# Loading q and k four units at a time, v's second slab by the batch, and identity made behind the first issues

## The chip, the cores and the metric

One core of a Trainium2 chip runs the whole program. The metric is the device time in microseconds of one execution; the median of three runs is compared. The profile is that of one execution, with its own time.

## The reference

Two stages, the output of the first being the input of the second. Batch 8, 8 heads, 576 positions, head size 64; chunks of 64 positions attend to themselves alone.

```python
scores = scale * np.matmul(q_c, k_c.transpose(0, 1, 2, 4, 3))   # per chunk: 64 x 64
scores = scores - np.max(scores, axis=-1, keepdims=True)
attn = np.exp(scores)
attn = attn / (np.sum(attn, axis=-1, keepdims=True) + 1e-09)
out = np.matmul(attn, v_c)                                      # per chunk: 64 x 64
...
x = out.transpose(0, 2, 1, 3).reshape(B, S, H * D)              # 8 x 576 x 512
wq = x @ w_q                                                    # 576 x 64
wk = x @ w_k
W_tok = scale * np.einsum('bsd,btd->bst', wq, wk)
mixed = np.einsum('bst,btd->bsd', W_tok, x)
return np.maximum(mixed, 0.0) @ w_out                           # 8 x 576 x 512
```

Inputs and output are float32 in HBM. The kernel works in float16 with float32 sums.

## The kernel before

**Units.** A batch has 8 heads of 9 chunks. The heads are taken in two slabs of four (slab 0: heads 0 to 3, slab 1: heads 4 to 7), so a batch has 36 chunk places, each with one chunk per slab. A unit is 8 places, that is 16 chunks; 36 units (`NU`) cover the 8 batches, and nine units cover a pair of batches. The fifth unit of the nine (`w == 4`) takes half of its places from each batch of the pair. v is cut otherwise: a batch has 18 slots of two places (`NS`), a unit uses four, and the two parts of a batch (`v_cuts`) hold slots 0 to 7 and 8 to 17.

**The loop.** Period `kk` of the main loop does, in the order in which the engines get it:

- `stage_b1(kk)`: TensorE computes the scores of unit kk (`sp`, L407), VectorE their row maximum (`mx`, L415). The pool of `sp` has one buffer.
- `stage_d1(kk-2)`: TensorE multiplies the transposed weights by v (`xp`, L452). v carries a column of ones, written by GpSimd's memset, so that the sum of the weights comes out as column 65.
- `fill(kk, 0, ...)`: steps of the second stage that a plan puts here.
- `stage_a1(kk+2)`: TensorE transposes q and then k of unit kk+2 (`tp`, L383, 16 instructions, eight for each). Then `loads(...)` gives GpSimd the loads that fall due.
- `stage_c(kk-1)`: TensorE transposes the exponentials (`ep`, L436); ScalarE copies them out (`et`).
- `stage_b2(kk)`: VectorE subtracts the maximum (`sh`, L421), ScalarE takes the exponential (`es`, L429).
- `stage_d2(kk-2)`: VectorE divides by the sum and writes `x_nat` (L464 to L467).
- `stage_a2(kk+2)`: VectorE copies the transposed q and k out of PSUM (`qkt`, L393).
- `fill(kk, 2, ...)`: steps of the second stage: transposes of `x_nat` (`tx`, L178), the products with w_q and w_k (L196), later the output product with w_out (`op`, L327), whose rows go out by SyncE.

A batch's second stage runs in the periods behind its attention. The first output product stands in period 13. Each engine works through its own instructions in program order and waits where an operand is not there.

**The loads.** All loads cast float32 to float16 and are issued by GpSimd, one queue, in program order. `load_qk(u)` loads unit u: one tile for q and one for k, each `[P, 2, R * D]`, one transfer of 128 KB each (256 rows of 512 bytes in float16); for the unit that straddles two batches, two transfers of 64 KB each. The tiles rotate over `AHEAD` = 8 buffers, so unit u waits until unit u-8 is transposed. `load_v(b, part)` loads a part of a batch's v: a memset of the ones, one transfer for slab 0 and two (the halves of the partitions swapped) for slab 1. Eight semaphores go round over GpSimd's transfers: a transfer is issued only when the eighth one before it has landed.

`wanted` holds all loads with the period at which each falls due; `loads(before)` issues those that are due before it. q and k of unit u are due at u-2, v's parts at two periods ahead of the unit that uses them first, w_q and w_k (`wqk16`) at 8, w_out (`wout16`) at 13; within a period v goes first, then q and k, then the weights:

```python
wanted = [(max(u - 2, 0), 1, load_qk, (u,)) for u in range(NU)]
...
wanted += [(8, 2, load_wqk, ()), (13, 2, load_wout, ())]
wanted.sort(key=lambda x: x[:2])
```

Identity (`ident`), which every transpose on TensorE reads, is made by two GpSimd instructions ahead of all loads.

Of the kernel before, what the change touches and what calls it, by code (L numbers as in the profile page):

```python
# [9 lines left out]
F16 = mybir.dt.float16  # L10
# [7 lines left out]
def kernel(  # L18
# [16 lines left out]
    nc = tc.nc  # L35
    B, H, S, D = q.shape
    DM = moe_w_out.shape[0]
    DH = moe_w_q.shape[1]
    CH = 64
    P = 128  # L40
    HQ = H // 2
    NC_ = S // CH
    NI = HQ * NC_
    NS = NI // 2
    NU = B * NI // 8
    W0 = 5 * CH
    R, G = 4, 16
    AHEAD = 8
# [2 lines left out]
    ds = bass.ds  # L51

    const = ctx.enter_context(tc.tile_pool(name="const", bufs=1))
    qn_pool = ctx.enter_context(tc.tile_pool(name="qn", bufs=AHEAD))
    v_pool = ctx.enter_context(tc.tile_pool(name="vpool", bufs=3))
    qkt_pool = ctx.enter_context(tc.tile_pool(name="qkt", bufs=3))
    sm_pool = ctx.enter_context(tc.tile_pool(name="smp", bufs=3))
# [12 lines left out]
    ctx.enter_context(tc.manual_schedule())  # L70

    ident = const.tile([P, P], F16, name="ident")
    make_identity(nc, ident[:])

    x_nat = const.tile([P, B * NS, 2, D], F16, name="x_nat")
    x_bat = x_nat[:].rearrange("p (b w s) l d -> p b w s l d", b=B, w=2)
# [1 line left out]
    wqk16 = const.tile([P, HQ, 2 * DH], F16, name="wqk16")  # L78
    wout16 = const.tile([P, HQ, DM], F16, name="wout16")

    v_cuts = ((0, 8), (8, NS))
    data = {}

    def load_qk(u):
        pair, w = divmod(u, 9)

        if w == 4:
            pieces = ((2 * pair, 32, 0, CH), (2 * pair + 1, 0, CH, CH))
        else:
            odd = int(w > 4)  # L90
            pieces = ((2 * pair + odd, 8 * w - NI * odd, 0, P),)
        for ti, x in enumerate((q, k)):
            tl = qn_pool.tile([P, 2, R * D], F16, name=f"qn{ti}", tag=f"qn{ti}")
            for b, i0, p0, pn in pieces:
                of = x[b].rearrange("h s d -> (h s) d").rearrange("(l p r) d -> p l (r d)", l=2, r=R)
                at = i0 * G
                nc.gpsimd.dma_start(tl[p0 : p0 + pn], of[at : at + pn])  # L97
            data[u, ti] = tl

    def load_v(b, part):  # L100
        n0, n1 = v_cuts[part]
        vt = v_pool.tile([P, 2, n1 - n0, D + 2], F16, name=f"vt{part}", tag=f"vt{part}")
        of = v[b].rearrange("h s d -> (h s) d").rearrange("(l n p) d -> l p n d", l=2, p=P)
        nc.gpsimd.memset(vt[:, :, :, D : D + 1], 1.0)

        for sl, to, at, rows in ((0, 0, 0, P), (1, 0, CH, CH), (1, CH, 0, CH)):
            nc.gpsimd.dma_start(vt[to : to + rows, sl, :, 0:D], of[sl, at : at + rows, n0:n1, :])  # L107
        data[b, part, 2] = vt

    def w_rows(w):  # L110
        return w.rearrange("(l i d) j -> l d i j", l=2, i=HQ)
# [10 lines left out]

    wanted = [(max(u - 2, 0), 1, load_qk, (u,)) for u in range(NU)]
    for b in range(B):
        for part in range(2):
            first = (NS * b + v_cuts[part][0]) // 4
            wanted.append((first + 2, 0, load_v, (b, part)))
    wanted += [(8, 2, load_wqk, ()), (13, 2, load_wout, ())]  # L130
    wanted.sort(key=lambda x: x[:2])

    def loads(before):
        while wanted and wanted[0][0] < before:
            _, _, load, args = wanted.pop(0)
            load(*args)

    loads(AHEAD - 2)

    drain = [False]  # L140
# [300 lines left out]
    def stage_d1(u):  # L441
        et = state[u]["et"]
        xp = x_psum.tile([P, 2, 512], F32, name="xp", tag="xp")
        xv = xp[:, :, 0 : 4 * 65].rearrange("p l (m e) -> p l m e", e=65)
        for m in range(4):
            b, s = divmod(4 * u + m, NS)
            part = s >= v_cuts[1][0]
            vt = data[b, part, 2][:, :, s - v_cuts[part][0]]
            for sl in range(2):
                for par in range(2):  # L450
                    at = CH * (par ^ sl)
                    nc.tensor.matmul(  # L452
                        xv[CH * par : CH * par + CH, sl, m, :],
                        lhsT=et[at : at + CH, m, CH * sl : CH * sl + CH],
                        rhs=vt[at : at + CH, sl, 0 : D + 1],
                        start=True,
                        stop=True,
                    )
        state[u]["xv"] = xv
# [21 lines left out]
    for b in range(B):  # L481
        period = lambda slots: -(-slots // 4) + 1
# [32 lines left out]
    for kk in range(NU - 1):  # L515
        stage_b1(kk)
        if kk >= 2:
            stage_d1(kk - 2)
        fill(kk, 0, 0.0)
        if 2 <= kk < NU - 2:  # L520
            stage_a1(kk + 2)
            loads(kk + 1 + AHEAD)
        if kk >= 1:
            stage_c(kk - 1)
        stage_b2(kk)
        if kk >= 2:
            stage_d2(kk - 2)
        if 2 <= kk < NU - 2:
            stage_a2(kk + 2)
        for u in ((1,), (2, 3))[kk] if kk < 2 else ():  # L530
            stage_a(u)
        fill(kk, 2, 1.4 if len(outs) < 4 else 1.9)
# [17 lines left out]
    u = NU - 1  # L550
    stage_b1(u)
    stage_d1(u - 2)
    stage_c(u - 1)
    stage_b2(u)
# [5 lines left out]
    chain(B - 2, 2)  # L560
    stage_c(u)
    stage_d1(u - 1)
    stage_d2(u - 1)
    put()
# [47 lines left out]
```

## Time and profile before

| | |
|---|---|
| runs | 150.97, 152.11, 152.70 us; median 152.11 |
| the profiled execution | 151.31 us, its span 149.5 us |
| TensorE's granted clock, mean | 0.957 |
| busy: TensorE (matmul) | 125.4 us, 84% of the span |
| busy: VectorE | 113.6 us, 76% |
| busy: ScalarE | 101.0 us, 68% |
| busy: GpSimd (POOL) | 98.0 us, 66% |
| GpSimd's loads of v (L107) | 48 transfers, 828 ns each |
| GpSimd's loads of q and of k (L97) | 40 and 40 transfers, 744 and 741 ns each |
| packets of GpSimd's queue | 58,976; 14.82 MB |

The span is the time from the first to the last instruction; the rest of an execution's time lies around it. GpSimd's busy time is that of issuing a transfer; the transfer lands some microseconds later. The page cuts the span into 40 slices of 3.74 us and gives each engine's busy share in tenths, so a 9 means 90% or more; the DMA row is the mean share of the 16 transfer engines. A timeline line gives start, duration, engine, line, operation, tiles written and read, and in brackets the idle time of the engine just before and what ended it.

### The profile page before, as it was taken

How to read it: one execution, taken by the hardware profiler on the slowest of the kernel's cores; microseconds unless marked ns; L12 is line 12 of the kernel's file. 1: busy time of each engine (PE TensorE's matmuls, PEld its weight loads, DVE VectorE, ACT ScalarE, POOL GpSimd, SP SyncE). 2: the span in 40 equal slices, each digit the busy share in tenths (PEclk: the TensorE clock that was granted, in tenths of full speed). 3: DMA queues.
4: the chain of work that ended last, by engine and by line, in shares of the span. 5: the costliest groups of instructions: out<-in, count | busy, mean ns of one | idle time of the engine just before them, and what ended most of it. 6: DMA issues, size and time to landing. Idle time of an engine off the chain costs nothing.

```text
span 149.5 us, 5958 instructions
## 1 busy us (share of the span) xinstructions
PE 125.4 (84%) x2516; PEld 84.5 (57%) x2516; DVE 113.6 (76%) x235; ACT 101.0 (68%) x199; POOL 98.0 (66%) x156
## 2 busy tenths in 40 slices
PE   0477898678789499999999999999899988999970
PEld 0256667556656265676756656765667554544430
DVE  0169998999999448998999899979989897354520
ACT  3013347368589529997898898879979996677130
POOL 7999999989999589879966997599650000000000
PEclk9999757999999869999999999999999999999996
DMA  2999999999999999999999999999999433234484
GB/s 19 140 149 158 140 158 154 162 90 139 164 136 141 170 181 199 224 215 201 219 172 226 188 199 246 221 163 227 208 215 138 129 147 148 76 140 119 167 269 153
DMA packets 64875, 25.09 MB, mean 168 GB/s; under 512 B 40784, under 2 KB 60368, under 8 KB 64848
## 3 DMA queue, kind: packets, MB, share of 16 engines
q0 software_dynamic: 58976, 14.82, 104.7%
q1 hardware_dynamic: 5728, 9.75, 19.3%
q8 instruction: 20, 0.33, 0.9%
q10 hardware_dynamic: 144, 0.13, 0.3%
q14 instruction: 7, 0.06, 0.1%
HBM read 29.62 MB, written 9.44 MB: 261 GB/s over the span
## 4 chain that ended last, share of the span: by engine, by line
PE 40%; POOL 17%; DVE 14%; ACT 13%; DMA 7%; issue 6%; DVEq 0%; ACTq 0%; POOLq 0%
PE op L327 13%; POOL qn L97 11%; PE tp L383 5%; DMA wout<-in_moe_w_out_dram 5%; POOL vt L107 4%; DVE sh L421 4%; PE ep L436 3%; DVE x_nat L467 3%; DVE mx L415 3%; PE sp L407 3%; ACT osb L154 3%; PE gp L250 3%; DMA qn<-in_k_dram 3%; ACT es L429 3%; PE tx L178 3%
## 5 line engine op out<-in xcount | busy, mean ns | idle before, releaser
L107 POOL DMA_DIRECT2D vt<-in_v_dram x48 | 38.1, 828 | 2.8 <-issue 1.8
L438 ACT COPY et<-ep 128x512 f16<-128x512 f16 x36 | 21.6, 600 | 19.2 <-PE ep L436 17.9
L383 PE MATMUL tp<-ident,qn 128*64 128x128 f16 x576 | 26.7, 239 | 7.7 <-DMA qn<-in_q_dram 4.8
L327 PE MATMUL op<-wout,rmx 128*128 128x512 f16 x124 | 31.4, 387 | 2.1 <-DMA wout<-in_moe_w_out_dram 1.9
L97 POOL DMA_DIRECT2D qn<-in_k_dram x40 | 29.4, 741 | 5.2 <-PE wpb L196 1.0
L97 POOL DMA_DIRECT2D qn<-in_q_dram x40 | 29.5, 744 | 3.0 <-DMA qn<-in_q_dram 0.9
L415 DVE TENSOR_REDUCE mx<-sp 128x8 f32<-128x512 f32 x36 | 24.7, 685 | 8.2 <-PE sp L407 8.2
L393 DVE COPY qkt<-tp 128x1024 f16<-128x1024 f16 x36 | 24.5, 682 | 6.7 <-PE tp L383 6.6
L429 ACT ACTIVATE es<-sh 128x512 f16<-128x512 f32 x36 | 23.4, 651 | 7.6 <-DVE sh L421 7.6
L421 DVE TENSOR_TENSOR sh<-sp,mx 128x512 f32<-128x512 f32 x36 | 24.9, 692 | 3.5
L383 PEld LDWEIGHTS <-qn 128*64 128x64 f16 x576 | 20.5, 120 | 12.3 <-DMA qn<-in_q_dram 4.8
L467 DVE TENSOR_TENSOR x_nat<-xp,rec 128x512 f16<-128x512 f32 x36 | 24.9, 692 | 1.2
L154 ACT COPY osb<-op 128x512 f32<-128x512 f32 (+1 forms) x29 | 17.1, 598 | 9.5 <-PE op L327 8.0
L407 PEld LDWEIGHTS <-qkt 64*64 64x64 f16 x576 | 12.8, 115 | 13.9 <-issue 4.9
L407 PE MATMUL sp<-qkt 64*64 64x64 f16 x576 | 17.0, 203 | 2.8 <-DVE qkt L393 1.9
L154 ACT COPY xt<-tx 128x768 f16<-128x768 f16 (+1 forms) x23 | 18.2, 790 | 0.9 <-PE tx L178 0.9
L327 PEld LDWEIGHTS <-rmx 128*128 128x128 f16 x124 | 11.2, 99 | 12.5 <-issue 3.2
L452 PE MATMUL xp<-vt,et 64*64 64x65 f16 x576 | 12.8, 201 | 5.5 <-DVE x_nat L467 2.6
L160 ACT ACTIVATE rmx<-ma 128x512 f16<-128x512 f32 x28 | 15.6, 622 | 0.1
L436 PE MATMUL ep<-ident,es 128*128 128x128 f16 x144 | 14.9, 229 | 0.0
L452 PEld LDWEIGHTS <-et 64*64 64x64 f16 x576 | 9.3, 110 | 7.3 <-ACT es L429 2.9
L178 PE MATMUL tx<-ident,x_nat 128*128 128x128 f16 x144 | 12.3, 223 | 0.0
(47 smaller groups left out, 141.4 us busy)
## 6 DMA issues: line engine op xcount, KB each, us to landing
out_dram<-osb SPq DMA_DIRECT2D x31, 256.0 KB, 3.5
qn<-in_q_dram POOLq DMA_DIRECT2D x32, 128.0 KB, 5.1
qn<-in_k_dram POOLq DMA_DIRECT2D x32, 128.0 KB, 5.4
vt<-in_v_dram POOLq DMA_DIRECT2D x8, 160.0 KB, 5.7
vt<-in_v_dram POOLq DMA_DIRECT2D x16, 80.0 KB, 5.4
out_dram<-osb SPq DMA_DIRECT2D x9, 128.0 KB, 2.4
vt<-in_v_dram POOLq DMA_DIRECT2D x8, 128.0 KB, 6.6
vt<-in_v_dram POOLq DMA_DIRECT2D x16, 64.0 KB, 5.9
```

The lines of the kernel that those rows point to most:

```text
L97: nc.gpsimd.dma_start(tl[p0 : p0 + pn], of[at : at + pn])
L107: nc.gpsimd.dma_start(vt[to : to + rows, sl, :, 0:D], of[sl, at : at + rows, n0:n1, :])
L154: (nc.vector.tensor_copy if on_vector else nc.scalar.copy)(to, of)
L327: nc.tensor.matmul(op[:], lhsT=rmx[:, i, ds(t * P, P)], rhs=wout16[:, i, :], start=(i == 0), stop=(i == HQ - 1),)
L383: nc.tensor.transpose(tp[CH * sl : CH * sl + CH, ti, :, r, :], src[:, sl, r * D : r * D + D], ident[:],)
L393: nc.vector.tensor_copy(qkt[:].rearrange("p t c k -> p (t c k)"), tp[:].rearrange("p t c r g -> p (t c r g)"),)
L407: nc.tensor.matmul(sp[rows, i ^ sl, :], lhsT=qkt[rows, 0, i, :], rhs=qkt[rows, 1, i, :], start=True, stop=True,)
L415: nc.vector.tensor_reduce(mx[:], sp[:], axis=AX.X, op=ALU.max)
L421: nc.vector.tensor_tensor(out=sh[:].rearrange("p i (g r) -> p i g r", g=G, r=R), in0=sp[:].rearrange("p i (r g) -> p i g r", g=G, r=R), in ...
L429: nc.scalar.activation(es[:], sh[:], AF.Exp, scale=scale_attn)
L452: nc.tensor.matmul(xv[CH * par : CH * par + CH, sl, m, :], lhsT=et[at : at + CH, m, CH * sl : CH * sl + CH], rhs=vt[at : at + CH, sl, 0 : ...
L467: nc.vector.tensor_tensor(out=x_nat[:, 4 * u : 4 * u + 4, :, :].rearrange("p m l d -> p l m d"), in0=xv[:, :, :, 0:D], in1=rec[:, :, :, No ...
```

## The change

- From unit 9 on (the third batch), q and k are loaded by fours: units 9 to 12, then 13 alone, 14 to 17, then 18 to 21, 22, 23 to 26, and so on. A group's tile is `[P, 2, 4, R * D]`, and one transfer brings one slab of four units of q or of k: 256 KB, 512 rows of 512 bytes. A group of four units is four transfers (q slab 0, q slab 1, k slab 0, k slab 1) in place of eight, and falls due when its first unit did before. Units 0 to 8 are still loaded one by one, into tiles of the same shape. The tiles of four rotate over three buffers; those of the straddling units have their own.
- v has one tile per batch. From the third batch on slab 1 is loaded whole, in two transfers (the two halves of the partitions, 18 slots each), with the first part of slab 0. The second part of slab 0 falls due where it did. There is one memset per batch.
- Unit 0's two transfers are issued ahead of identity's two instructions; the other loads follow behind these.

With that the issue order behind unit 8 becomes: units 9 to 12; v of batch 1, second part; w_q and w_k; v of batch 2, first part of slab 0 and slab 1 whole; unit 13; units 14 to 17; v of batch 2, second part of slab 0; w_out; v of batch 3 likewise; units 18 to 21; and so on. Before it was: unit 9; v of batch 1, second part; unit 10; w_q and w_k; units 11 and 12; v of batch 2, first part; units 13 and 14; v of batch 2, second part; unit 15; w_out; unit 16; and so on.

```diff
-    qn_pool = ctx.enter_context(tc.tile_pool(name="qn", bufs=AHEAD))
+    qn_pool = ctx.enter_context(tc.tile_pool(name="qn", bufs=3))
...
     ident = const.tile([P, P], F16, name="ident")
-    make_identity(nc, ident[:])
...
-    def load_qk(u):
+    def load_qk(u, n):
         pair, w = divmod(u, 9)
-        if w == 4:
-            pieces = ((2 * pair, 32, 0, CH), (2 * pair + 1, 0, CH, CH))
-        else:
-            odd = int(w > 4)
-            pieces = ((2 * pair + odd, 8 * w - NI * odd, 0, P),)
         for ti, x in enumerate((q, k)):
-            tl = qn_pool.tile([P, 2, R * D], F16, name=f"qn{ti}", tag=f"qn{ti}")
+            if w == 4:
+                tl = qn_pool.tile([P, 2, 1, R * D], F16, name=f"qm{ti}", tag=f"qm{ti}")
+                pieces = ((2 * pair, 32, 0, CH), (2 * pair + 1, 0, CH, CH))
+            else:
+                odd = int(w > 4)
+                if w in (0, 5):
+                    tiles[ti] = qn_pool.tile([P, 2, 4, R * D], F16, name=f"qn{ti}", tag=f"qn{ti}")
+                at = w - 5 * odd
+                tl = tiles[ti][:, :, at : at + n]
+                pieces = ((2 * pair + odd, 8 * w - NI * odd, 0, P),)
             for b, i0, p0, pn in pieces:
                 of = x[b].rearrange("h s d -> (h s) d").rearrange("(l p r) d -> p l (r d)", l=2, r=R)
-                at = i0 * G
-                nc.gpsimd.dma_start(tl[p0 : p0 + pn], of[at : at + pn])
-            data[u, ti] = tl
+                g0 = i0 * G
+                if n == 1:
+                    nc.gpsimd.dma_start(tl[p0 : p0 + pn, :, 0], of[g0 : g0 + pn])
+                    continue
+                for sl in range(2):
+                    nc.gpsimd.dma_start(
+                        tl[:, sl], of[g0 : g0 + n * P, sl].rearrange("(t p) x -> p t x", p=P)
+                    )
+            for j in range(n):
+                data[u + j, ti] = tl[:, :, j]
-    def load_v(b, part):
-        n0, n1 = v_cuts[part]
-        vt = v_pool.tile([P, 2, n1 - n0, D + 2], F16, name=f"vt{part}", tag=f"vt{part}")
+    def load_v(b, sl, n0, n1):
+        if not (sl or n0):
+            data[b] = v_pool.tile([P, 2, NS, D + 2], F16, name="vt", tag="vt")
+            nc.gpsimd.memset(data[b][:, :, :, D : D + 1], 1.0)
...
-    wanted = [(max(u - 2, 0), 1, load_qk, (u,)) for u in range(NU)]
+    wanted = [(max(u - 2, 0), 1, load_qk, (u, 1)) for u in range(9)]
+    for u in range(9, NU, 9):
+        wanted += [(u + w - 2, 1, load_qk, (u + w, n)) for w, n in ((0, 4), (4, 1), (5, 4))]
     for b in range(B):
-        for part in range(2):
-            first = (NS * b + v_cuts[part][0]) // 4
-            wanted.append((first + 2, 0, load_v, (b, part)))
+        for part, (n0, n1) in enumerate(v_cuts):
+            period = (NS * b + n0) // 4 + 2
+            wanted.append((period, 0, load_v, (b, 0, n0, n1)))
+            if b < 2:
+                wanted.append((period, 0, load_v, (b, 1, n0, n1)))
+            elif part == 0:
+                wanted.append((period, 0, load_v, (b, 1, 0, NS)))
...
+    load_qk(*wanted.pop(0)[3])
+    make_identity(nc, ident[:])
     loads(AHEAD - 2)
```

More of the change, by code (lines that the diff above doesn't have):

```diff
@@ L81 @@
     v_cuts = ((0, 8), (8, NS))
-    data = {}
-    def load_qk(u):
+    data, tiles = {}, {}
+    def load_qk(u, n):
         pair, w = divmod(u, 9)
-        if w == 4:
-            pieces = ((2 * pair, 32, 0, CH), (2 * pair + 1, 0, CH, CH))
-        else:
-            odd = int(w > 4)
-            pieces = ((2 * pair + odd, 8 * w - NI * odd, 0, P),)
-        for ti, x in enumerate((q, k)):
-            tl = qn_pool.tile([P, 2, R * D], F16, name=f"qn{ti}", tag=f"qn{ti}")
+        for ti, x in enumerate((q, k)):
+            if w == 4:
[8 more added lines that the diff above has]
+                pieces = ((2 * pair + odd, 8 * w - NI * odd, 0, P),)
@@ L103, in load_v @@
+                for sl in range(2):
[8 more added lines that the diff above has]
+            nc.gpsimd.memset(data[b][:, :, :, D : D + 1], 1.0)
         of = v[b].rearrange("h s d -> (h s) d").rearrange("(l n p) d -> l p n d", l=2, p=P)
-        nc.gpsimd.memset(vt[:, :, :, D : D + 1], 1.0)
@@ L106, in load_v @@
-        for sl, to, at, rows in ((0, 0, 0, P), (1, 0, CH, CH), (1, CH, 0, CH)):
-            nc.gpsimd.dma_start(vt[to : to + rows, sl, :, 0:D], of[sl, at : at + rows, n0:n1, :])
-        data[b, part, 2] = vt
+        for to, at, rows in ((0, CH, CH), (CH, 0, CH)) if sl else ((0, 0, P),):
+            nc.gpsimd.dma_start(
+                data[b][to : to + rows, sl, n0:n1, 0:D], of[sl, at : at + rows, n0:n1, :]
+            )
     def w_rows(w):
@@ L446, in stage_d1 @@
             b, s = divmod(4 * u + m, NS)
-            part = s >= v_cuts[1][0]
-            vt = data[b, part, 2][:, :, s - v_cuts[part][0]]
+            vt = data[b][:, :, s]
             for sl in range(2):
```

## The prediction

> **What bounds the kernel now.** I read the slices first, then VectorE's timeline, then the chain of waits at the gaps, then the issue and transfer rows of the loads.
>
> ```profile
> DVE  0169998999999448998999899979989897354520
> POOL 7999999989999589879966997599650000000000
> DMA  2999999999999999999999999999999433234484
> ```
>
> The DMA engines are busy from the first microseconds to about 115 us; GpSimd (POOL), which issues every load, is full until 45 us. VectorE is at 9 or more in most slices, with a hole at slices 13 and 14. Its timeline there (start, duration, line, count, idle before):
>
> ```profile
> 47.18 0.68 DVE L415 TENSOR_REDUCE mx<-sp 128x8 f32<-128x512 f32 x1
> 47.97 0.69 DVE L421 TENSOR_TENSOR sh<-sp,mx 128x512 f32<-128x512 f32 x1
> ...
> 49.61 0.68 DVE L393 COPY qkt<-tp 128x1024 f16<-128x1024 f16 x1
> 54.10 0.69 DVE L415 TENSOR_REDUCE mx<-sp 128x8 f32<-128x512 f32 x1 [3.80 <-PE sp L407]
> ```
>
> One L415 runs per unit, so I call its start for unit u mx(u). mx(12) is at 44.16, mx(13) at 47.18, a pitch of 3.03 us in which VectorE never rests: that is the loop's bound. mx(14) comes 3.80 us late. The chain of waits says why:
>
> ```profile
> 44.62 6.87 DMA wout<-in_moe_w_out_dram
> 51.49 0.14 issue
> 51.62 1.86 PE op L327 x4
> 53.49 0.46 PE sp L407 x6
> ```
>
> TensorE works in program order. It had finished everything ahead of L327 at 49.73, waited 1.89 us for the output weights, which land at 51.49, and only then reached unit 14's scores. With the weights there, L327 takes 0.86 us (its row at 56.28), so mx(14) would have come at about 51.05: the late weights cost 3.0 us. After that mx(17) is at 63.62 and no later group of rows waits for a load. The 30 us behind the loop are not touched.
>
> The margin of the loads is small everywhere:
>
> ```profile
> 28.90 0.64 PE L383 MATMUL tp<-ident,qn 128*64 128x128 f16 x16
> 29.47 0.40 PE L436 MATMUL ep<-ident,es 128*128 128x128 f16 x4
> 29.70 0.50 PE L178 MATMUL tx<-ident,x_nat 128*128 128x128 f16 x6
> 30.55 0.44 PE L407 MATMUL sp<-qkt 64*64 64x64 f16 x16 [0.35 <-DVE sh L421]
> ```
>
> Unit 9 is transposed (L383) at 28.90, its k half at 29.2. Its k was issued at 23.02 and, by the 4.7 us that loads take there, is in SBUF at 27.6. Three rows price the transfer engines (window, us; busy us and counts by engine; clock; DMA share; GB/s):
>
> ```profile
> 24.90:26.50 1.60, 1.10 (x46) 0.81 (x42) 1.60 (x3) 1.44 (x3) 1.60 (x4) 1.00 1.24 154
> 45.60:51.50 5.90, 3.80 (x83) 2.62 (x81) 4.45 (x11) 4.65 (x11) 4.88 (x8) 0.98 1.14 147
> 54.00:56.00 2.00, 2.00 (x50) 1.65 (x43) 1.73 (x5) 0.48 (x2) 1.27 (x3) 0.82 1.48 191
> ```
>
> 154 GB/s where q and k alone move behind a short queue, 191 behind a full one, 147 around the output weights.
>
> **Identity.** Its two GpSimd instructions take 0.74 to 1.44 and now stand behind unit 0's two issues. Unit 0's q goes out 0.70 us sooner; TensorE's first transpose, at 4.59 before, starts at 3.9, and identity is ready at 0.74 + 2 x 0.71 + 0.70 = 2.9. If that cover of 1.0 us were gone, the first transpose would slip by what is missing. Every later issue keeps its time. The gain ends at unit 6, still issued at 16.48:
>
> ```profile
> 16.48 4.00 DMA qn<-in_k_dram
> 20.48 0.04 issue
> 20.52 0.64 PE tp L383 x8
> ...
> 22.95 0.70 DVE mx L415
> ```
>
> mx(5) hangs on that landing, and its time does not change. Bounds 0 and -0.7; I take 0.
>
> **GpSimd's issues.** Twenty-four units lose 8 transfers per four (0.71 us apart) and get 4 of 512 rows each. No row shows a 512-row q or k transfer. Bounds: 0.71 (a 256-row transfer) and 1.42 (twice that); v's 640-row transfers take 0.72 and its 1280-row one 0.98, so 0.77. Six batches lose four v half transfers (2 x 0.69, 2 x 0.72) and get two of about 0.84. Together 24 x 1.42 - 24 x 0.77 + 6 x 1.14 = 22 us less on GpSimd, and eight memsets of 0.24 fewer. On the path that is worth nothing by itself: after unit 8 the transfer engines set the pace, at either bound of the price. The tile waits do not bind either: units 18 to 21 reuse the tile of 5 to 8, transposed long before.
>
> **The move.** Up to unit 8 both orders are the same; its k is issued at 21.60 and lands 4.7 us later, at 26.3. Behind it now come units 9 to 12 as four transfers, 1.05 MB, and unit 9's k half waits for the last one, three units' bytes more than before. At 172 GB/s, halfway between 154 and 191 (the queue is now deeper than in the first row), that is 6.1 us: landing 32.4, against a need at 29.2. TensorE stops in front of L383 for 3.2 us; queued behind it are L436, L178 and unit 8's L407. From the landing these need 0.3 + 0.4 + 0.5 + 0.44 us; at unit 6 the same steps took 2.47, so I take 2.0: mx(8) at 34.4, not 32.04, a loss of 2.4. The slab-0 rest of v of batch 1, then wqk, land behind the group, at about 34.3 and 35.1, where TensorE now needs them at 34.1 and 35.2: no second wait beyond a few tenths.
>
> Next is wout. Ahead of it: v of batch 1 (0.33 MB), wqk (0.13), v of batch 2 without the end of slab 0 (0.43), unit 13 (0.26), units 14 to 17 (1.05), the end of slab 0 (0.16): 2.36 MB, 13.7 us; wout itself 0.52 MB at 147 GB/s, 3.6 us. It lands at 49.7; TensorE wants it at 49.73 + 2.4 = 52.1. So the wait of 1.89 goes, and mx(14) = 47.18 + 2.4 + 3.03 + 0.85 = 53.5, against 54.10: 0.6 us gained. Units 14 to 17 land at about 45.1, needed at 44.6 + 2.4.
>
> Next is the group 18 to 21. Behind wout come 0.43 MB of v and 1.05 MB: 0.7 MB until 53.9, when stores begin, and then 0.75 MB with two stores of 0.26 at about 205 GB/s (between 192 and 209, what 51.5 to 61.5 and 61.5 to 95.1 moved): 6.2 us, landing 60.1. Unit 18's k is needed 2.35 us ahead of mx(17), at 60.6. At 165 GB/s in place of 172 the same steps give 61.2 to 62.5 (two or three stores) and mx(17) between 63.6 and 64.9. The later groups have margins of 1 to 3 us on the same count.
>
> Sum at mx(17): between -0.65 and +1.2 us, middle +0.3. Profiled execution: 151.31 us (span 149.5, 1.8 around it), so 151.6; the median of the runs, 152.11, is 0.8 above it: **152.4 us**, no change within 1%, which is about what a measurement of this kernel can tell.
>
> **Rivals.** *The groups land late (slower).* Place: TensorE in front of L383 of units 9 and 18. Price: at 150 GB/s units 9 to 12 land at 33.3 (mx(8) +3.3), wout at 52.7, just in time, units 18 to 21 at about 64, and mx(17) = 66.3, +2.7; 0.1 to 0.3 more at a later group. It decides below about 160 GB/s. For it: 154 and 147 above, and the waits of TensorE for q and k that are there already. Against: those rows had short queues, or the output weights in them. Time 155.1.
>
> *The queue runs full (faster).* At 191 GB/s units 9 to 12 land at 31.8 (mx(8) +1.8), wout at 47.8, units 18 to 21 before they are needed: mx(14) is 1.25 early and stays so. With 0.5 us less chain behind the landing (1.5 by the sum of its rows) it is 1.75. For it: the row of 191, and that GpSimd no longer starves the queue between 26 and 45 us. Against: that rate held for 2 us. Time 150.5.
> [...]
>
> *The change does not do what it says:* a 512-row issue costs 1.42 or more. Then the fourth transfer is issued at 22.3 + 3 x 1.42 = 26.6 and lands, at 4.7 + 0.7 us, at 32.0, inside the forecast; it is part of it.
>
> **Chances.** Forecast 0.39, slower rival 0.37 (154 to 156), faster rival 0.24 (149.8 to 150.6). The forecast's own range is 151.0 to 153.6. Taking in both rivals' prices and the runs' spread (150.97 to 152.7): 149.9 to 156.0. So faster by over 1%: 0.24, within 1%: 0.39, slower by over 1%: 0.37.
>
> **What would show it.** Right: TensorE waits about 3 us for qn near 29 to 32 us and mx(8) is at 34 to 35; no wait for wout; mx(14) at 53 to 54; GpSimd busy about 76 us. The first transpose at 3.9 with mx(5) still near 22.9. Wrong: units 9 to 12 land before 30 (no wait), or a wait of over 2 us before unit 18, or L327 waiting for wout again.

## The result, and the profile after

The changed kernel takes 159.94 us (median of 4 runs, 159.11 to 160.69) against 152.19 us (4 runs, 150.97 to 152.70) on the same chip: ratio 1.053, 95% interval 1.045 to 1.060. It is slower by 5%, outside the range of the prediction. The profiled execution took 159.11 us, its span is 157.3 us, 7.8 more than before. Here and below, ratios are of the undisturbed runs on both sides, so they can differ a little from the ratio of the medians.

The slices of the page of after:

```profile
DVE  0378889927799788978793799988998997535630
POOL 7999999669973783677663469100000000000000
PEclk9999999965999999999996999999999999999997
DMA  3999999999999999999999999997121333243574
```

GpSimd has the room that was forecast (74.7 us busy instead of 98.0), and the transfer engines are as full as before, but for less long: the last load lands at 108.6 us, 115.3 before. VectorE, which set the pace, now has deep holes at slices 8 and 21 and shallow ones at 9, 10, 13, 17 and 19 (the first slice is slice 0). The clock falls at slices 8, 9 and 21. The starts of L437 (the old L415, `mx`) on VectorE's timeline show where the holes come from; the columns are start, duration, what it is, and in brackets the idle time before it:

```profile
35.58 0.69 DVE L437 TENSOR_REDUCE mx<-sp 128x8 f32<-128x512 f32 x1 [1.06 <-PE sp L429]
...
40.11 0.69 DVE L437 TENSOR_REDUCE mx<-sp 128x8 f32<-128x512 f32 x1 [1.41 <-PE sp L429]
...
53.33 0.69 DVE L437 TENSOR_REDUCE mx<-sp 128x8 f32<-128x512 f32 x1 [0.99 <-PE sp L429]
...
56.89 0.69 DVE L437 TENSOR_REDUCE mx<-sp 128x8 f32<-128x512 f32 x1 [0.44 <-PE sp L429]
...
80.74 0.68 DVE L437 TENSOR_REDUCE mx<-sp 128x8 f32<-128x512 f32 x1
...
87.09 0.69 DVE L437 TENSOR_REDUCE mx<-sp 128x8 f32<-128x512 f32 x1 [2.34 <-PE sp L429]
```

These are units 8, 9, 13, 14, 21 and 22. Before, they were at 32.04, 35.07, 47.18, 54.10, 76.38 and 79.41. So 3.5 us are lost at unit 8, 1.5 more at unit 9, some is won back at 14, and 3.3 are lost at 22. Each time TensorE is what VectorE waits for. TensorE's timeline at the first loss:

```profile
29.25 0.24 PE L405 MATMUL tp<-ident,qn 128*64 128x128 f16 x1
30.10 0.41 PE L405 MATMUL tp<-ident,qn 128*64 128x128 f16 x7 [0.60 <-DMA qn<-in_q_dram]
31.43 0.24 PE L405 MATMUL tp<-ident,qn 128*64 128x128 f16 x1 [0.92 <-DMA qn<-in_k_dram]
33.16 0.63 PE L405 MATMUL tp<-ident,qn 128*64 128x128 f16 x7 [1.49 <-DMA qn<-in_k_dram]
...
35.69 1.07 PE L405 MATMUL tp<-ident,qn 128*64 128x128 f16 x16
```

Unit 9 waits three times (for q's second slab and for each slab of k) for the four transfers of units 9 to 12, until 33.16. Then the same row of 16 transposes takes 1.07 us where it took 0.64: the granted clock is 0.50 from 33.5 to 36 us and 0.57 on average from there to 40 us, and for this while TensorE, not VectorE, sets the pace. The output weights, late before, are waited for no more. What comes after that has no load in its brackets:

```profile
49.30 0.25 PE L405 MATMUL tp<-ident,qn 128*64 128x128 f16 x2
51.03 0.58 PE L405 MATMUL tp<-ident,qn 128*64 128x128 f16 x14 [1.48 <-issue]
...
57.25 0.28 PE L473 MATMUL xp<-vt,et 64*64 64x65 f16 x11 [0.34 <-issue]
...
64.46 0.32 PE L473 MATMUL xp<-vt,et 64*64 64x65 f16 x16 [1.36 <-DVE mx L437]
...
80.88 0.58 PE L405 MATMUL tp<-ident,qn 128*64 128x128 f16 x14
83.72 0.30 PE L405 MATMUL tp<-ident,qn 128*64 128x128 f16 x2 [2.26 <-issue]
...
84.35 0.47 PE L218 MATMUL wpa<-xt,wqk 128*128 128x320 f16 x1
```

At 83.72 TensorE stops in the middle of a row of transposes of data that had been there for long (14 of its 16 were done), and "issue" says that no semaphore released it. At 51.03 it stops so too, ahead of transposes of unit 14's q, which had landed at 46.06; but of this unit's k the second slab lands only at 50.66, so a wait of about 1 us for k would have stood there without the stop. The stop at 64.46 bears the name of VectorE's `mx`, but L473 does not read `mx`; it is of the same kind (below). Behind the longest one the clock is halved again (L218 takes 0.47 us, 0.30 before). The same place before:

```profile
76.52 0.64 PE L383 MATMUL tp<-ident,qn 128*64 128x128 f16 x16
77.09 0.40 PE L436 MATMUL ep<-ident,es 128*128 128x128 f16 x4
77.33 0.30 PE L196 MATMUL wpa<-xt,wqk 128*128 128x320 f16 x1
```

Counted over all of TensorE's instructions in the trace (weight loads, matmuls and the few of its sequencer), these four stops and one of 0.36 us at 75.92 have 1473, 1729, 1985, 2753 and 2497 instructions before them: exactly 256 apart, or a multiple of it. (The pairs 747, 876, 1005 and 1391 of an expectation below are the matmuls and the sequencer's instructions counted together, to within one; the matmuls alone are 726, 853, 980 and 1362.) The page's queues have a row that fits:

```profile
q8 instruction: 20, 0.33, 0.8%
...
qn<-in_k_dram POOLq DMA_DIRECT2D x12, 256.0 KB, 8.4
vt<-in_v_dram POOLq DMA_DIRECT2D x12, 144.0 KB, 10.1
```

The row of q8 is twenty packets of 16,384 bytes (0.33 MB) of instructions, 64 bytes for each of 256; the page counts them with the loads, as a share of the same 16 transfer engines. TensorE has 5077 instructions in this trace, 19.8 times 256. The packets that start at 48.32, 54.72, 61.70 and 81.42 end 1.3 to 1.6 us before the four stops do. The last two of these rows are the median time from issue to landing: k's groups and v's take 8 to 10 us, where single units took 5.4 before and v's parts 5.4 to 6.6. The queue of loads beside an instruction packet is deeper than it was: by the issues and landings in the trace, up to 1.1 MB of loads (1 MB is 1024 KB here) were on their way before, and up to 1.6 or 1.7 MB in the 8 us ahead of each of these four packets.

### The profile page after: what moved, and what is told of

It is laid out like the page before. It is cut to its first block, busy times and chain, and to the rows that moved or that the text cites. A ratio compares the mean times of both kernels' runs of the same rounds, so it can differ in the third digit from the quotient of the medians.

```text
span 157.3 us, 5872 instructions
## 1 busy us (share of the span) xinstructions
PE 129.1 (82%) x2516; PEld 87.9 (56%) x2516; DVE 114.4 (73%) x235; ACT 101.6 (65%) x199; POOL 74.7 (47%) x112
## 4 chain that ended last, share of the span: by engine, by line
PE 45%; POOL 15%; DVE 14%; DMA 9%; ACT 8%; issue 6%; DVEq 0%; ACTq 0%; POOLq 0%
PE op L349 13%; POOL qn L103 7%; PE tp L405 6%; DMA qn<-in_k_dram 5%; POOL vt L119 4%; PE ep L458 4%; DVE x_nat L488 4%; DVE sh L443 4%; DMA wqd<-wqkT 3%; DVE mx L437 3%; PE tx L200 3%; PE wpa L218 3%; PE sp L429 3%; PE xp L473 2%; PE wknp L253 2%
## 5 line engine op out<-in xcount | busy, mean ns | idle before, releaser
L405 PE MATMUL tp<-ident,qn 128*64 128x128 f16 x512 | 25.2, 246 | 11.9 <-DMA qn<-in_q_dram 5.4
L437 DVE TENSOR_REDUCE mx<-sp 128x8 f32<-128x512 f32 x36 | 24.7, 687 | 12.6 <-PE sp L429 12.5
L119 POOL DMA_DIRECT2D vt<-in_v_dram x36 | 31.1, 905 | 5.0 <-DMA vt<-in_v_dram 2.0
L415 DVE COPY qkt<-tp 128x1024 f16<-128x1024 f16 x36 | 24.6, 683 | 9.1 <-PE tp L405 9.0
L349 PE MATMUL op<-wout,rmx 128*128 128x512 f16 x124 | 30.5, 379 | 0.2 <-ACT rmx L182 0.2
L405 PEld LDWEIGHTS <-qn 128*64 128x64 f16 x512 | 19.3, 124 | 15.9 <-DMA qn<-in_q_dram 5.9
L473 PE MATMUL xp<-vt,et 64*64 64x65 f16 x576 | 13.8, 204 | 6.5 <-DVE x_nat L488 2.8
L458 PE MATMUL ep<-ident,es 128*128 128x128 f16 x144 | 16.0, 241 | 0.0
L473 PEld LDWEIGHTS <-et 64*64 64x64 f16 x576 | 10.0, 112 | 8.2 <-ACT es L451 2.9
L200 PE MATMUL tx<-ident,x_nat 128*128 128x128 f16 x144 | 13.2, 233 | 0.4 <-issue 0.4
L106 POOL DMA_DIRECT2D qn<-in_q_dram x12 | 9.4, 813 | 4.4 <-DMA qn<-in_k_dram 1.9
L106 POOL DMA_DIRECT2D qn<-in_k_dram x12 | 9.1, 777 | 4.8 <-PE gp L272 1.0
```

The costliest lines, as they stand in the source:

```text
L119: nc.gpsimd.dma_start(data[b][to : to + rows, sl, n0:n1, 0:D], of[sl, at : at + rows, n0:n1, :])
L349: nc.tensor.matmul(op[:], lhsT=rmx[:, i, ds(t * P, P)], rhs=wout16[:, i, :], start=(i == 0), stop=(i == HQ - 1),)
L405: nc.tensor.transpose(tp[CH * sl : CH * sl + CH, ti, :, r, :], src[:, sl, r * D : r * D + D], ident[:],)
L415: nc.vector.tensor_copy(qkt[:].rearrange("p t c k -> p (t c k)"), tp[:].rearrange("p t c r g -> p (t c r g)"),)
L437: nc.vector.tensor_reduce(mx[:], sp[:], axis=AX.X, op=ALU.max)
L458: nc.tensor.transpose(ep[:, m, :], es[:, 2 * m : 2 * m + 2, :], ident[:])
```

## Experiments

The account up to the end of the loop, from the starts of `mx` in each profiled execution (us; the last column is the difference of the two before it):

| kernel | unit 9 | unit 14 | unit 17 | unit 35 | 17 to 35 |
|---|---|---|---|---|---|
| before | 35.07 | 54.10 | 63.62 | 120.72 | 57.10 |
| after | 40.11 | 56.89 | 67.51 | 128.37 | 60.86 |
| before, with q and k by fours alone | 39.50 | 55.38 | 65.39 | 128.27 | 62.88 |
| fours in unit order, 128 KB | 40.54 | 55.68 | 65.59 | 123.80 | 58.21 |
| order of after, 128 KB | 40.18 | 55.33 | 65.48 | 122.85 | 57.37 |
| due by unit, 128 KB | 35.72 | 51.97 | 61.98 | 119.73 | 57.75 |
| after, two buffers | 38.95 | 55.96 | 66.00 | 127.89 | 61.89 |
| after, at most 1 MB on its way | 40.92 | 58.55 | 72.27 | 130.08 | 57.81 |

### The parts alone

Identity moved behind unit 0's issues, nothing else:

```diff
-    make_identity(nc, ident[:])
...
+    load_qk(*wanted.pop(0)[3])
+    make_identity(nc, ident[:])
     loads(AHEAD - 2)
```

> Kernel before with nothing but identity moved behind unit 0's issues. Theory: the first transpose starts 0.1 to 0.7 us sooner, mx(5) stays between 22.5 and 23.3, the time stays at 151.5 to 153. Rival (the move itself costs, by pushing unit 1's loads): mx(5) later by over 0.7 us and over 1 us on the time.

Measured 153.58 us (10 runs) against 153.01 (13), ratio 1.006 [0.998, 1.013]: nothing that these runs can tell. The first transpose is at 4.50, `mx` of unit 5 at 23.6 (22.95 before), a little later than either bound of the theory.

v's slab 1 by the batch, nothing else (the lines of `load_v`, `wanted` and `stage_d1` of the change):

> Kernel before with nothing but v's part of the change. Group theory (the loss comes from q and k by fours): 151 to 154 us, L327 still waiting for wout. Rival (v's slab 1 whole, with 1152 rows in a transfer, holds up the rest): over 156 us, TensorE waiting for q or k or for its instructions.

Measured 152.87 us (4 runs, 150.98 to 154.97) against 153.01: no loss that four runs can tell. L327 still waits 0.75 us for w_out, and no stop without a semaphore is over 0.3 us.

q and k by fours, nothing else (the lines of `load_qk`, the pool and `wanted` for q and k):

> Kernel before with nothing but q and k by fours. Group theory: most of the loss of the whole change, 156 to 161 us, with TensorE waiting about 3.5 us for unit 9 and mx(8) at 35 to 36. Rival (v's part makes the loss): 151 to 154 us.

Measured 158.97 us, ratio 1.037 [1.025, 1.048]. Unit 8's `mx` is at 36.30, and a stop without a semaphore (2.27 us in brackets) ends at 82.69 in a row of transposes. Six stops of over 0.5 us stand at multiples of 256 instructions from those of after. Most of the loss is in this part.

### What in the fours costs: order or size

The group's transfers in the order of units (unit 9's q, its k, unit 10's q, ...), eight of 128 KB:

```diff
-                for sl in range(2):
-                    nc.gpsimd.dma_start(
-                        tl[:, sl], of[g0 : g0 + n * P, sl].rearrange("(t p) x -> p t x", p=P)
-                    )
+        for j in range(n):
+            for ti, x in enumerate((q, k)):
...
+                    nc.gpsimd.dma_start(tl[p0 : p0 + pn, :, 0], of[g0 : g0 + pn])
```

> Changed kernel with the same tiles, places and due times, but each group of four sent as eight transfers of 128 KB in the order of the units (q and k of the first unit, then of the second). Group theory: unit 9 has its own data first, its wait goes, mx(8) at 32 to 33. Theory of the instruction blocks (TensorE's 16 KB blocks of instructions come late behind GpSimd's queue, which holds up to 8 transfers of 256 KB): with half the bytes in the queue the waits of TensorE without a semaphore go too, 149 to 152.5 us. Rival (it is the order of the bytes and not the size of the transfers that holds up the blocks): mx(8) at 32 to 33, but waits of 1 to 2.5 us at block ends stay, 153 to 157 us.

Measured 155.32 us, ratio 1.016 [1.006, 1.025]. Unit 8 is on time (32.53), but unit 9 comes at 40.54, as late as in after. TensorE now waits for v, which stands behind the whole group in the queue:

```profile
35.13 0.26 PE L467 MATMUL xp<-vt,et 64*64 64x65 f16 x2 [2.71 <-DMA vt<-in_v_dram]
35.72 0.32 PE L467 MATMUL xp<-vt,et 64*64 64x65 f16 x6 [0.32 <-DMA vt<-in_v_dram]
35.97 1.06 PE L399 MATMUL tp<-ident,qn 128*64 128x128 f16 x16
```

The wait has moved from k to v, and the slow clock follows it (1.06 for the row of 16). So the first loss is that of the due time: 1.05 MB fall due at once, and whatever was put behind them is late. The stops at block ends are down to 0.53 us at most; both the theory's time and the rival's stops of 1 to 2.5 us were missed.

Units 9 to 12 one by one again, and the fours from unit 14 on:

```diff
-    wanted = [(max(u - 2, 0), 1, load_qk, (u, 1)) for u in range(9)]
+    wanted = [(max(u - 2, 0), 1, load_qk, (u, 1)) for u in range(13)]
...
+            if u + w > 12
```

> Changed kernel, but units 9 to 12 still come one by one, in the order of the kernel before; fours from unit 14 on. Theory (the first group costs 5 us at mx(9), the late output weights took 3 of them back): mx(9) at 35 to 36, then L327's wait for wout is back with 2 to 4 us, and the later waits of TensorE at block ends stay: 155.5 to 159 us. Rival (the first group is the whole loss): 150 to 153.5 us.

Measured 158.12 us, ratio 1.041 [1.036, 1.046]; its one profile is of an execution of 175.69 us at a mean granted clock of 0.70, so the waits that were expected are not shown. Without the first group most of the loss is still there.

The order of after (q of four units, then k of four) in transfers of 128 KB, and each unit's transfers due with the unit, in tiles of four:

> The kernel after with its order of loads kept (q of four units, then k of four units, due with the first unit), but each group sent as eight transfers of 128 KB, one unit each, instead of four of 256 KB. With the eight semaphores of GpSimd's transfers at most eight are on their way, so the bytes in flight are halved (about 1.0 MB at most instead of 1.4 to 2). Theory A (late blocks of instructions come from the bytes queued ahead of them): units 9 to 12 still late (k of unit 9 is the fifth transfer instead of the fourth of double size; it lands about 31.5 to 32.5, mx(8) 34 to 35), but the stops of TensorE without a semaphore in the middle of a row of transposes (2.43 us at 83.7, 1.59 at 51.0, 1.16 at 64.5 in the kernel after) shrink to under 1 us each; time about 155 to 157.5, ratio 1.02 to 1.035. Theory B (the order in which units become available is the whole matter, the size of a transfer nothing): stops of over 1.5 us stay, time 158.5 to 160 as after.

> The kernel after with identity's move and v's slab 1 by the batch kept and tiles of four units kept, but q and k of each unit sent as two transfers of 128 KB and due with that unit, as in the kernel before. Theory A (the loss is in the due times and the size of the groups alone; identity, v and the larger tiles cost nothing): ratio 1.00 within 0.01, about 152 to 153.5 beside a kernel before of 152; mx(8) within 0.6 of 32.0, no stop of TensorE without a semaphore over 0.5 us. Rival (the parts that cost nothing alone, identity 1.006 and v 0.999, cost something together, or the tiles of four bind): over 1.01, 153.8 or more.

The first took 154.28 us, ratio 1.012 [1.007, 1.017]; the second 153.84 us, ratio 0.996 [0.990, 1.002]. With the due times of before, and identity, v and the tiles of after, little or nothing is left of the loss: its twelve runs spread from 150.18 to 155.65, their median is 1.0% above that of before (152.25) and just meets the rival's 153.8, so 1% is not excluded. In its profile (150.18 us) one stop of 0.53 us at a block end and `mx` of unit 8 at 32.69 are a little over what theory A allowed. With the due times and the order of after but half the size, the loss at unit 9 is whole (40.18 against 40.11, now 1.41 for k and 1.17 and 0.40 for v, at half clock), but behind it the loop runs as before: no stop without a semaphore is over 0.75 us (the loads on their way peak at 1.3 MB, where w_out is among them), and units 17 to 35 take 57.37 us instead of 60.86. The time was a little under what theory A gave. So of the 5% some 1 is due time and order, and some 4 come with the transfers of 256 KB and the deeper queue that they make.

### What the stops are

Twenty spare transposes at the start of after, which move every later instruction by 20 pairs:

```diff
+    spare = bank([P, 8, P], F16, name="spare")
+    for j in range(20):
+        nc.tensor.transpose(spare[:, j % 8, :], ident[:], ident[:])
```

> Changed kernel with 20 more transposes of identity on TensorE ahead of unit 0, into a tile that nobody reads. The waits of TensorE without a semaphore fell at its pairs (weight load and product) 747, 876, 1005 and 1391 of the program. Theory of the instruction blocks (256 instructions or 128 pairs each): the waits that are there stay at 747, 876, 1005, 1391 within 4, counted with the 20 new pairs, so they hit work that stood 20 pairs earlier. Rival (late data): they move with the work, to 767, 896, 1025, 1411.

One execution, 159.37 us. The stops on TensorE's timeline:

```profile
61.34 0.82 PE L349 MATMUL op<-wout,rmx 128*128 128x512 f16 x3 [1.15 <-issue]
...
68.87 0.37 PE L458 MATMUL ep<-ident,es 128*128 128x128 f16 x2 [2.27 <-issue]
69.03 0.47 PE L218 MATMUL wpa<-xt,wqk 128*128 128x320 f16 x1
...
82.54 0.22 PE L473 MATMUL xp<-vt,et 64*64 64x65 f16 x2 [0.55 <-issue]
```

Counted with the spare ones they have 1985, 2241 and 2753 instructions before them; two smaller ones at 101.19 and 108.02 (0.48 and 1.24 us) have 3521 and 3777. All five are on the grid of 256 that the stops of after are on, and 1985 and 2753 are the very places of two of them, now on other work (the second of four products with w_out; at 68.87 it is the third of four transposes of `es`). The stops at 1473 and 1729 are gone and three others are new, so the place is fixed to the grid, while at which of its points a stop falls changes. Late data would have stayed with its line. What fits is instructions that come late: in after their packets end 1.3 to 1.6 us before the stops.

Two buffers for q and k instead of three, meant to make the queue shorter:

```diff
-    qn_pool = ctx.enter_context(tc.tile_pool(name="qn", bufs=3))
+    qn_pool = ctx.enter_context(tc.tile_pool(name="qn", bufs=2))
```

> Changed kernel with two instead of three buffers for the tiles of four units, so that from units 18 to 21 on GpSimd waits for TensorE and its queue is shorter; transfers and order are the same. Theory of the instruction blocks (they come late behind a long queue): the waits without a semaphore behind 60 us go or halve, loads land in 5 to 8 us instead of 8 to 12, 155.5 to 158.5 us. Rival (the size of the transfers, not the length of the queue, delays the blocks): same waits, 159 to 161 us. Second rival (the loads now come late): waits for qn of units 23 or 27, over 160 us.

Measured 158.82 us against 151.97. The loads still land 8.4 us (k) behind their issue, and up to 1.8 MB are on their way, so the queue was no shorter and this tells nothing of its length. The stop at 2753 is there again, 2.53 us long.

So the length was set directly. The transfers and the order of after, but before a load that would bring the bytes on their way over 1 MB, GpSimd reads one element of the load that must have landed:

```diff
+    def dma(to, of, kb, free):
...
+        last = None
+        while sum(x for x, _ in flying) + kb > 1024:
+            _, last = flying.pop(0)
+        if last is not None:
+            lo, view = last
+            nc.gpsimd.tensor_copy(seen[lo : lo + view.shape[0], :], view)
+        nc.gpsimd.dma_start(to, of)
+        flying.append((kb, free))
```

> The kernel after with its order and its 256 KB transfers kept; only the number of bytes on their way is held at 1 MB or less: before it issues a load that would exceed it, GpSimd copies one element of the youngest load that must have landed by then. Computation and data are otherwise those of the kernel after. Theory A (the late blocks of instructions come from the bytes queued ahead of them, 1.3 to 1.6 MB in the kernel after): the stops of TensorE without a semaphore at the block boundaries (2.43, 1.59 and 1.16 us in the kernel after) shrink to under 0.8 us each; units 9 to 12 are late as before (mx(8) 35 to 36, mx(9) about 40); time 154 to 156, ratio 1.01 to 1.025, as with transfers of 128 KB in the same order. Theory B (a transfer of 256 KB by itself holds up the fetch of instructions, however few are queued): stops of over 1.5 us stay, 158 us or more. If GpSimd's waits starve the transfer engines, TensorE waits for q, k or v instead, which would be seen as waits with a load as releaser.

Measured 160.64 us, ratio 1.063 [1.055, 1.072]. The two halves of theory A part. The long stops are gone, with transfers of 256 KB: the one that is left has 0.58 us (at 116.96), the row where 2.26 us stood has no bracket and is whole, and units 17 to 35 take 57.81 us. But the time is not 154 to 156, because the queue now runs short ahead of unit 18:

```profile
65.94 0.24 PE L431 MATMUL tp<-ident,qn 128*64 128x128 f16 x1 [0.69 <-DMA qn<-in_k_dram]
68.14 0.63 PE L431 MATMUL tp<-ident,qn 128*64 128x128 f16 x7 [1.96 <-DMA qn<-in_k_dram]
...
85.69 0.64 PE L431 MATMUL tp<-ident,qn 128*64 128x128 f16 x16
86.26 0.40 PE L484 MATMUL ep<-ident,es 128*128 128x128 f16 x4
```

`mx` of unit 17 comes 7.54 us after that of 16. With the deep queue of after the instructions are held up (a stop of 2.26 us); with this shallow one the groups of four are late (a wait of 1.96 us). Theory B (a transfer of 256 KB, however few are queued) falls.

How the bytes on their way bear on the blocks can be read from the profiles (all but that of the run in which units 9 to 12 come one by one; the first block of each is left out). At the stops, TensorE goes on 1.2 to 1.7 us after the packet with its next block has ended; a packet takes 0.9 to 2.0 us; and a block of 256 instructions lasts 5.3 to 6.6 us in most of the loop of before. What is left is how long after TensorE has entered one block the packet of the next one starts:

| loads on their way as TensorE enters the block (1 MB = 1024 KB) | blocks | median, us | lowest and highest |
|---|---|---|---|
| none | 36 | 0.3 | -0.7, 1.9 |
| up to 0.5 MB | 27 | 1.4 | 0.1, 2.6 |
| 0.5 to 0.75 MB | 51 | 2.1 | 0.9, 4.1 |
| 0.75 to 1.0 MB | 57 | 3.1 | 0.4, 5.1 |
| over 1.0 MB | 45 | 3.8 | 2.0, 5.8 |

The more is on its way, the later the packet starts, by some 3 us for each MB. By an estimate from these figures (5.3 to 6.6 us, less 1 for the packet and 1.4 behind it) a start later than about 3 to 4 us leaves a stop. So these figures show no threshold, and the bytes do not say all: with q and k by fours alone the stop of 2.27 us stands behind 1.1 to 1.25 MB, while in the order of after in 128 KB up to 1.3 MB gave 0.75 us, and with two buffers one block at 1.6 MB came in time. At 1.0 to 1.25 MB the latest start was 5.4 us with q and k in 256 KB and 3.95 us in 128 KB; whether the size of a transfer adds something of its own is not shown.

### What the late output weights were worth

The kernel before, with its first output product one period later, when the weights are there:

```diff
-        while outs and outs[0][0] == place and spent + outs[0][1] <= budget:
+        while kk > 13 and outs and outs[0][0] == place and spent + outs[0][1] <= budget:
```

> Kernel before, with the first output product one period later (14 instead of 13), so that TensorE doesn't wait there for wout. By the 3.0 us that the late weights cost: mx(14) at 50 to 51.5 and 148 to 150.5 us. Rival (the wait only moves to the next place, or the product comes back at the end): 151 to 153 us.

Measured 152.25 us (12 runs) against 151.97 (17), ratio 1.001 [0.998, 1.004]. `mx` of unit 14 comes at 51.05, exactly where the prediction put it without the wait, but TensorE, which had waited 1.19 us for k at 49.16 and runs at half clock from 49.90 to 53.32, then waits for the next loads:

```profile
52.73 1.17 PE L383 MATMUL tp<-ident,qn 128*64 128x128 f16 x16 [0.30 <-DMA qn<-in_q_dram]
...
62.83 0.41 PE L383 MATMUL tp<-ident,qn 128*64 128x128 f16 x8 [1.01 <-DMA qn<-in_q_dram]
```

Of the 3.05 us won at unit 14, 0.36 are left at unit 32 (111.44 against 111.80); there a stop of 0.94 us at a block end (113.24) takes the rest, and unit 35 is at 121.51, 120.72 before. In this order the stream of loads itself was a bound of the kernel; the wait for w_out was only where it showed.

## Why the prediction was wrong, step by step

Measured at the end of the loop the loss is 128.37 - 120.72 = 7.65 us. It splits into 5.04 at unit 9, -3.35 at unit 14 (the pitch from 13 to 14 is 3.56 instead of 6.91) and 5.96 for the rest. Of this, 3.32 come at unit 22, behind the longest stop and at its slow clock, 1.10 at unit 13 (the stop at 51.03), 0.88 at unit 17 (the one at 64.46), and the others are smaller.

- **The bound.** Right that the loop runs at 3.03 us a unit on VectorE and that the margin of the loads is small. Wrong in worth: "the late weights cost 3.0 us" holds for the place, not for the time, as the kernel before with a later product shows. In after the wait did go, and its 3.35 us did count, because TensorE was by then 5 us late and the loads had caught up.
- **Identity.** Nil, as forecast. The working was off: the first transpose is at 4.52, not 3.9, since GpSimd's first issue comes at 1.25 and not right behind its constants:

```profile
1.25 0.82 POOL L103 DMA_DIRECT2D qn<-in_q_dram  x1 [0.80 <-POOLq L617]
2.06 0.73 POOL L103 DMA_DIRECT2D qn<-in_k_dram  x1
```

- **GpSimd's issues.** Right: 74.7 us busy (76 forecast); a load of 512 rows is issued in 0.74 us at the least, and in the median in 0.74 (k) and 0.79 (q; 0.77 taken). As said, it is worth nothing on the path.
- **The group of units 9 to 12.** Place right, size wrong. Landing 33.12 instead of 32.4: 1.05 MB in 6.75 us (156 GB/s, not 172), near the row of 154. From landing to `mx` 2.46 us instead of 2.0. Together `mx` of unit 8 at 35.58, 34.4 forecast. A missing term is the clock: 1.5 us more at unit 9 because TensorE works at half speed after the wait. The row for it was in the profile of before, where L327 took 1.86 us behind a wait of 1.89 and 0.86 without; the prediction used it for w_out and not for the wait that it created.
- **The output weights.** No wait, as forecast. But they land at 54.01 instead of 49.7, and TensorE came for them at 55.45 only because it was late itself; `mx` of unit 14 is at 56.89, not at 53.5. The 172 GB/s failed most here. Units 14 to 17 land at 50.66 instead of 45.1: 2.20 MB in 17.5 us, 125 GB/s. GpSimd could not keep the queue filled: the loads issued at 30.34, 31.67 and 33.40 went out 0.3 us after the landings of the group's last three transfers (30.05, 31.39 and 33.12), each the eighth before, and from 33.1 to 36.7 us the transfer engines moved 91 GB/s. Unit 14's k half was wanted at about 49.6, so this group was late as well. With 1 MB at most on its way, where no stop stands before it, that wait shows:

```profile
52.04 0.41 PE L431 MATMUL tp<-ident,qn 128*64 128x128 f16 x7 [1.12 <-DMA qn<-in_k_dram]
```

- **The group of units 18 to 21.** Landing 63.04 instead of 60.1, no wait all the same, since unit 18 is transposed at 64.9. So the slower rival was right on the rate and on unit 9 and wrong on unit 18; its price, 155.1, is that of another sum. The faster rival had neither its 191 GB/s nor its time.
- **"The later groups have margins of 1 to 3 us".** This is the step that failed. It looked at the data alone, and put the wait for instructions at nothing. The page counts the packets of instructions among those of the same transfer engines (q8, 0.33 MB), and with the deeper queue (up to 1.7 MB on its way instead of 1.1), which the faster rival counted as a gain ("GpSimd no longer starves the queue"), they came late: most of the 5.96 us, of which about 1 at unit 13 would have been a wait for k without the stop. No row of before showed a stop of this kind, and the prediction let that stand for a deeper queue too.
- **The size of the transfers.** The group took 6.75 us from unit 8's k in transfers of 256 KB, and 7.49 us in the same order in 128 KB: a factor of 1.1.

What remains open: why an instruction packet starts later while loads of another queue are on their way, what beside the bytes makes a block late (the starts scatter by 3 us at the same depth), and when a stop halves the clock. The runs show that the packets start later with more bytes on their way, not what makes them.

## What to carry to other kernels

Fewer and larger loads took work from the engine that issues them (GpSimd is busy for 74.7 us instead of 98.0), which is worth something only if that engine sets the pace; they also made the first unit of a group wait for the last (unit 9 until 33.16 us), and whatever was queued behind the group (the output weights land at 54.01 us, 51.49 before). Before deepening a queue of loads, ask what else goes through the transfer engines: stops of TensorE in the middle of a row, a multiple of 256 instructions apart and released by nothing, were instructions that came late here. And when a wait goes away, look for the next wait on the same stream before counting it as a gain.

## What the runs showed of the hardware

**Instruction blocks came late behind loads.** Blocks of 16 KB, 256 instructions each, came up to 2.53 us too late for TensorE (two buffers) in the kernels that had q and k in 256 KB and 1.6 to 1.8 MB of loads on their way at the peak; with a peak of 1.0 (the held queue), 1.1 (before, and before with the later product) or 1.3 MB (in 128 KB) no stop of this kind was over 0.94 us. The page of after counts twenty of them, and the stops lie 256 instructions or a multiple of that apart. In the kernel before no such stop was over 0.3 us, in after the longest had 2.26 us.

**The clock was halved behind some stops.** Behind a stop of TensorE of 2.26 us the granted clock was 0.50 for 3 us, and the matmuls took half as long again and more (0.47 instead of 0.30 us); behind one of 1.48 us it stayed full (the next rows of L218 take 0.30). Windows of after (us, busy us and counts by engine, clock, DMA share, GB/s), ahead of the long stop, in it and behind it:

```profile
79.80:81.40 1.60, 1.54 (x52) 1.01 (x50) 1.60 (x3) 1.60 (x4) 0.85 (x1) 1.00 1.40 230
81.40:84.00 2.60, 0.34 (x6) 0.16 (x4) 1.68 (x5) 0.91 (x2) 0.94 (x2) 0.96 1.33 242
84.00:87.00 3.00, 3.00 (x46) 2.00 (x48) 0.69 (x1) 1.81 (x4) 1.10 (x2) 0.50 1.47 230
```

The slow stretches last 3.41 us or twice that (83.78 to 87.19 and 32.58 to 39.41 in after, 51.30 to 54.72 in before). They begin within 0.6 us of the end of a single stop of 1.89 us (the wait for w_out before) or 2.26 us, or of the last of three waits of 0.60, 0.92 and 1.49 us close together (unit 9 in after). Not every such stop has one: behind those of 2.27 us (q and k by fours alone) and 2.53 us (two buffers) at the same place the clock stayed full.

```profile
82.70:86.00 3.30, 3.22 (x77) 2.38 (x78) 1.91 (x3) 2.28 (x7) 2.70 (x5) 1.00 1.36 234
82.60:86.00 3.40, 3.32 (x80) 2.50 (x80) 2.04 (x4) 2.41 (x7) 1.45 (x2) 1.00 1.37 231
```

There unit 22 came 1.9 and 2.2 us late, and 3.3 us in after, where the clock was halved. What decides between the two is not shown.
